# Sending inverse sums to DRAM as single elements from ScalarE's queue, without the transpose and the copy, and with all places planned anew

## The chip, the core and the metric

The kernel runs on one core of a Trainium2 chip. The metric is the device time of one execution in microseconds, as the median of several runs. A core has five engines with queues of their own: TensorE (PE, with its weight loads shown as PEld), VectorE (DVE), ScalarE (ACT), GpSimd (POOL) and SyncE (SP), and 16 DMA engines that move data between DRAM and the on-chip memory.

## What is computed

Top-k attention, then a block that expands, applies a softmax-gated unit, normalises and contracts (all float32; the two weight matrices and the gain arrive as float64).

```python
# q, k, v: (8, 8, 576, 64)
scores = scale * np.matmul(q, k.transpose(0, 1, 3, 2))
kth = np.partition(scores, -32, axis=-1)[..., -32:-31]
scores = np.where(scores >= kth, scores, -1000000000.0)
attn = np.exp(scores - np.max(scores, axis=-1, keepdims=True))
attn = attn / (np.sum(attn, axis=-1, keepdims=True) + 1e-09)
x = (attn @ v).transpose(0, 2, 1, 3).reshape(4608, 512)
h = x @ w_in                                   # 512 -> 1024
solu = h * softmax(h)
ln = (solu - mean(solu)) / np.sqrt(var(solu) + 1e-06) * g_ln
return ln @ w_out                              # 1024 -> 512
```

## The kernel before

Work is cut into 32 attention steps and 36 token groups of 128 rows. A step takes one batch and four chunks of 128 queries of two heads each, with a fifth chunk of the 64 remaining queries of both heads, so nine tiles of 128 x 576 scores. Their names: `scores` (PE) multiplies queries and keys in two row tiles of 64 rows; `evac` (ACT) copies the result from PSUM to the tile X; `count0`, `count1`, `nearest`, `best` and the `merged` stages (ACT and DVE) find the 32nd largest value; `exps` (ACT) makes E; `keep` (DVE) sets what is under the 32nd value to zero and sums each row into `den_all`; `transpose_p` (PE) and `copy_p` (ACT) turn E into PT; `attn_v` and `attn_t` (PE) multiply by the values into `om`; `copy_v` (DVE) multiplies `om` by the inverse sums and writes x, transposed. A token group then runs `mm1` (PE), `hexp` (ACT), `solu` (DVE), `square` (ACT), `spread` and `ln` (POOL), `transpose_ln` (PE), `copy_ln` (ACT), `mm2` (PE), `store` (ACT) and `send` (SP). The weights are converted from float64 at the start (`w_bits`, `w_corr` on DVE, `w_sum` on PE, `w_copy` on ACT) and read once more near the end for a check of their exponents (`w_again`, `w_exp`, `w_check`).

The way of the inverse sums is what the change touches. `inverse` (DVE) writes `rden`, 128 queries x 9 tiles. `copy_v` needs them along the free axis and the same in 64 partitions for each head, since `om` is transposed. The first three steps (`QUICK`) do this on PE (`spread_r`) and ACT (`copy_s`). The other 29 go through DRAM: `turn_r` (PE, line 2438) transposes `rden` to 9 x 128 into a `tp` buffer of PSUM, `copy_r` (ACT, line 2442) copies it into the tile `scales`, `rd_out` (SP, line 2447) stores the nine rows of 128 floats to the DRAM tile `rows`, and `rd_in` (SP, line 2456) loads them back in four broadcasts to 64 partitions each.

PSUM buffers are scarce: two of `tp` (all transposes), two of `big` (scores and mm1), two of `o` (attn_v, mm2, estimates). There is one `scales` buffer.

The order is written out ahead. `work_of` lists every operation with its engine, its cost in ns on that engine, what it comes after, which buffers it uses and how long after its start it is complete (`late`). `PLACES` gives each operation a rank. `arranged` goes through time and, on each engine, chooses among the operations that can start within `PATIENCE` of the earliest the one with the smallest rank. `TURN` is what it counts for PE's change between full-array work ("f"), row tiles ("r") and column tiles ("c"). The order that comes out is emitted as it is: each engine executes its own list in order, and semaphores hold it where data or buffers are not ready.

Of the kernel before, what the change touches and what calls it, by code (L numbers as in the profile page):

```python
# [8 lines left out]
F32 = mybir.dt.float32  # L9
# [6 lines left out]
P = 128  # L16
# [426 lines left out]
class Work:  # L443
# [6 lines left out]
    def add(self, key, engine, ns, after=(), uses=(), late=0, mode=None):  # L450
# [7 lines left out]
TURN = {("r", "f"): 150, ("f", "r"): 180, ("c", "f"): 205, ("f", "c"): 145,  # L458
        ("r", "c"): 180, ("c", "r"): 180}
# [34 lines left out]
def work_of(B, NP, steps, NF, w_wide):  # L494

    NM, NT = 4, 9
# [13 lines left out]
    for b in range(B):  # L510
        for hp in range(NP):
            n = pair(b, hp)
            add(("load_k", n), "SP", 950, behind("load_k", n), [("km", n)], late=2300)
# [11 lines left out]
    for i, (b, chunks) in enumerate(steps):  # L525
# [3 lines left out]
        add(("load_q", i), "SP", 1150, behind("load_q", i), [("q", i)], late=2300)  # L529
# [51 lines left out]
        if i in QUICK:  # L581
            for part in range(2):
                add(("spread_r", i, part), "PE", 436 if part else 654, [("inverse", i)],
                    [("small", i), ("tp", (i, "r", part))], mode="c")
                add(("copy_s", i, part), "ACT", 252 if part else 360, [("spread_r", i, part)],
                    [("tp", (i, "r", part)), ("rb", i)], 140)
        else:
            add(("turn_r", i), "PE", 109, [("inverse", i)], [("small", i), ("tp", (i, "r"))], mode="f")
            add(("copy_r", i), "ACT", 157, [("turn_r", i)], [("tp", (i, "r")), ("rb", i)], 135)
            add(("rd_out", i), "SP", 550, [("copy_r", i)], [("rows", i), ("rb", i)], 2200)  # L590
            add(("rd_in", i), "SP", 2200, [("rd_out", i)], [("rows", i), ("rb", i)], 3000)
# [108 lines left out]
def arranged(work, rank):  # L700
# [23 lines left out]
    while len(start) < len(ops):  # L724
# [56 lines left out]
        -339758, -12781, -25208, -27877, 37731, 233358, 296, 105051, 96218, 90025, 178978, 252902,  # L781
        244000, 268551, 386938, 415275, 391135, 450403, 490825, 467595, 536751, 620389, 565976,
        679127, 740719, 661851, 783898, 770731, 790228, 893927, 893785, 963266,
    ],
    "load_t": [
        -80025, -31145, 36300, 49546, 49494, 80911, 88940, 148972, 157187, 191399, 204618, 265303,
        242814, 379090, 332469, 458214, 479052, 406643, 515896, 540675, 515666, 668938, 671843,
        720581, 717982, 793192, 742027, 827758, 819520, 890032, 913039, 961682,
    ],
    "load_v": [  # L790
        5319, 1480, 51022, 45481, 188816, 144910, 179523, 153830, 308475, 246135, 333153, 327154,
        412030, 463265, 437640, 432012, 583103, 575722, 599884, 559552, 638124, 712663, 704767,
        749478, 828294, 823974, 856710, 843393, 969577, 973661, 982483, 1008016,
    ],
    "prep_t": [
        -61945, -87345, 26278, 19638, -8730, 123415, 112043, 64876, 197393, 203082, 209099,
        243285, 345702, 316325, 405050, 432741, 494037, 489994, 501941, 520044, 617082, 642835,
        681846, 688123, 761106, 717329, 792500, 787155, 909850, 920002, 957331, 948603,
    ],
    "prep_tc": [  # L800
        4338, 31729, 74439, 103211, 71892, 81529, 72919, 101742, 164515, 194340, 295053, 275591,
        364723, 341559, 415389, 407627, 461137, 438553, 503629, 486164, 631436, 665358, 673210,
        709654, 759555, 758129, 786441, 814781, 916829, 948853, 939851, 972581,
    ],
    "prep_k": [
        -60943, -63278, -70349, -26069, -42273, -8750, 127523, 59000, 243742, 222705, 246805,
        237589, 361575, 400598, 401099, 421797, 472374, 488858, 508262, 574786, 637110, 675577,
        651769, 709906, 752064, 690701, 778193, 843688, 919829, 948201, 942202, 976495,
    ],
    "prep_kc": [  # L810
        4386, 1259, 123243, 137096, 118230, 85986, 126740, 91080, 220993, 187701, 233433, 204820,
        376470, 380016, 398731, 436516, 487070, 463318, 479133, 561124, 640742, 660501, 650085,
        710914, 775148, 783534, 778524, 835240, 922803, 1013798, 954303, 988974,
    ],
    "key_square": [
        -4807, -10479, 66029, 137082, 107576, 118285, 100863, 99055, 254747, 223927, 219983,
        241887, 382074, 399900, 389837, 454608, 479887, 488157, 529275, 515189, 644860, 690979,
        690863, 719751, 737841, 761871, 779678, 864903, 916172, 907344, 975895, 1000571,
    ],
    "tail_square": [  # L820
        26929, 14605, 100013, 137131, 136063, 58308, 80392, 79370, 239575, 272229, 246883, 251581,
        308867, 311986, 422199, 446864, 515800, 468069, 496456, 535239, 638456, 682141, 683618,
        672660, 775588, 750923, 772211, 791047, 855138, 930345, 971291, 966358,
    ],
    "key_stats": [
        92348, -19748, 26035, 15202, 122190, 113992, 181544, 108957, 246207, 243025, 253021,
        288772, 408504, 419434, 373738, 411187, 494000, 466874, 543467, 571921, 654056, 667583,
        687366, 699046, 765262, 778703, 806677, 825191, 868806, 1026195, 947557, 979604,
    ],
    "load_q": [  # L830
        -59271, -10584, 162877, 208999, 217746, -8934, 78975, 113377, 212835, 187676, 290008,
        301140, 284434, 326724, 436860, 497003, 414204, 458642, 518992, 564916, 579785, 620846,
        720192, 679914, 758251, 783803, 740037, 850815, 909964, 906235, 929596, 981195,
    ],
    "prep_q": [
        -52938, -38118, 56938, 77044, -59554, 85219, 162709, 142989, 215771, 247729, 278667,
        316160, 380350, 357086, 442926, 462694, 491000, 518228, 547128, 562615, 640425, 655851,
        698990, 730851, 735544, 760091, 823699, 888865, 908286, 923741, 969433, 1014055,
    ],
    "prep_qc": [  # L840
        5438, 63366, 52446, 134767, 64136, 75161, 195035, 183808, 242849, 287460, 293191, 371510,
        425968, 364349, 488763, 476329, 465356, 525184, 499437, 614146, 626301, 699742, 698545,
        745735, 768636, 779604, 840926, 877014, 945804, 930997, 952200, 1033695,
    ],
    "query_square": [
        63169, 84418, 69142, 92064, 62677, 75066, 191341, 120686, 227118, 285294, 276140, 342226,
        401444, 383473, 418081, 451775, 479613, 516395, 563335, 580962, 631937, 667102, 657175,
        748447, 762133, 776709, 773949, 878639, 892717, 939130, 971775, 1057944,
    ],
    "estimate": [  # L850
        -83506, 127952, 79019, 27039, 105930, 180710, 89736, 42838, 243394, 306540, 313101,
        342801, 413707, 436191, 458562, 488897, 502885, 576495, 566964, 582618, 653574, 699822,
        722473, 753711, 782087, 850158, 856146, 880647, 959006, 991084, 1003644, 1011006,
    ],
    "length": [
        55390, 64287, 21492, 142925, 91820, 89828, 187422, 189102, 225343, 302444, 316321, 331213,
        430746, 450075, 467065, 483618, 443843, 521081, 600380, 589002, 638944, 706432, 747530,
        730429, 775752, 832366, 866032, 877201, 961113, 983506, 1018506, 1066670,
    ],
    "root": [  # L860
        99246, 101551, 133489, 76502, 153437, 159993, 328449, 258282, 273277, 322044, 312402,
        345682, 435376, 421796, 426558, 489636, 494032, 574332, 622205, 621698, 663835, 788227,
        724548, 699723, 787574, 869704, 806750, 895189, 992785, 957593, 981899, 1024982,
    ],
    "begin": [
        11137, 56722, 26318, 141798, 82875, 187369, 201720, 176412, 273406, 321410, 278640,
        361581, 425447, 451800, 489085, 488954, 519027, 611009, 600940, 647109, 684366, 701264,
        752228, 758419, 793179, 851495, 882821, 921112, 988338, 1009069, 981779, 1020470,
    ],
    "scores": [  # L870
        [-59418, -45149, -46228, -36187, -85715, -39882, -83465, -59766, -61961],
        [82657, 60941, 68216, 26269, 63090, 61996, 26242, 61177, 58723],
        [87860, 87901, 87890, 62437, 67835, 57982, 159959, 48482, 69765],
        [84367, 83743, 155862, 144031, 34877, 75359, 128841, 135567, 145817],
        [71537, 53849, 68902, 132976, 59114, 118037, 68873, 110264, 107915],
        [141646, 97925, 94716, 134455, 142943, 99507, 191485, 186882, 96824],
        [152938, 191224, 59110, 197551, 203891, 215510, 127964, 202152, 197201],
        [226026, 229460, 237313, 237035, 187502, 187736, 192780, 199624, 198798],
        [269141, 275943, 254553, 254580, 277300, 269126, 277259, 275937, 249924],
# [358 lines left out]
        787847, 845540, 871626, 909493, 924810, 1042553, 1016671, 1060191, 1094822, 1099148,  # L1238
    ],
    "spread_r": [  # L1240
        [61416, 70137],
        [85209, 91923],
        [131370, 129488],
    ],
# [539 lines left out]
def fast_path(  # L1784
# [29 lines left out]
    NM = 4  # L1814
# [929 lines left out]
```

## Time and profile before

| | |
|---|---|
| median of 3 runs | 1195.1 us (1193.06 to 1195.21) |
| profiled execution | 1193.35 us |
| its span, first to last instruction | 1191.5 us |
| granted TensorE clock, mean | 0.991 |
| PE, DVE, ACT, POOL busy | 1143.5, 1054.0, 1014.4, 154.4 us |
| DMA packets | 110408, 64.55 MB |
| `rd_out`, the store of nine rows, on SP | 29 issues, 300 ns each (median) |
| `rd_in`, the broadcasts, on SP | 116 issues, 588 ns each (median) |
| `inverse`, first reciprocal, on DVE | 32, 196 ns each (mean) |

The profile is of one execution. A group's row gives line, engine, operation, the tiles written and read, the shapes and the count; then the busy time in us and the mean duration of one in ns; then the time for which the engine was idle just before these instructions, and what ended it. Matmuls overlap in the array, so the duration of one is longer than the distance between two starts; the timeline's start times give the distance. DMA-issuing instructions appear on the queue of the engine that issues them (SPq) and do not count as busy; the time of the record is that of the issue, and the landing comes later.

### The profile page before, as it was taken

The numbers are of one execution on the slowest core, as the hardware profiler recorded it, in microseconds if no ns is written. First come the engines' busy times: TensorE is split into PE (matmuls) and PEld (weight loads), VectorE is DVE, ScalarE is ACT, GpSimd is POOL, SyncE is SP. The second block draws the span as 40 slices with busy tenths as digits, with TensorE's granted clock in tenths as the row PEclk, the third lists the DMA queues.
The fourth block names the chain that finished last, engine by engine and source line by source line (L and its number), as shares of the span: only waits on it lengthen the run. The fifth ranks groups of instructions, "written<-read, shape, count | busy, mean of one in ns | idle before, by whom it ended". The sixth has DMA issues, their size and how long they took to land.

```text
span 1191.5 us, 18863 instructions
## 1 busy us (share of the span) xinstructions
PE 1143.5 (96%) x5868; PEld 648.2 (54%) x5868; DVE 1054.0 (88%) x3113; ACT 1014.4 (85%) x2180; POOL 154.4 (13%) x169
## 2 busy tenths in 40 slices
PE   6689999999999999999999999999999999999997
PEld 3345455555555555555555655555555555555553
DVE  4999999999899999899979998899989888999821
ACT  7899798999988898999896998999877989988642
POOL 1101101102021020202031010211013001120110
PEclk9799999999999999999999999999999999999999
DMA  7323111012110122111120112111020101102521
GB/s 202 97 75 92 43 34 48 13 49 54 59 26 28 33 63 65 37 45 40 51 54 12 40 49 68 31 41 52 30 76 18 42 21 40 59 11 91 173 76 30
DMA packets 110408, 64.55 MB, mean 54 GB/s; under 512 B 89421, under 2 KB 97882, under 8 KB 110298
## 3 DMA queue, kind: packets, MB, share of 16 engines
q1 hardware_dynamic: 110298, 63.25, 18.8%
q8 instruction: 49, 0.80, 0.3%
q14 instruction: 61, 0.50, 0.1%
HBM read 53.65 MB, written 9.57 MB: 53 GB/s over the span
## 4 chain that ended last, share of the span: by engine, by line
PE 50%; DVE 27%; ACT 17%; issue 3%; POOL 2%; DMA 0%; DVEq 0%; ACTq 0%; POOLq 0%
PE o_ps L2628 14%; PE h_ps L2567 9%; PE s_ps L2216 9%; ACT sg L2291 7%; PE tp_p L2470 6%; PE om L2526 6%; DVE junkv L2234 6%; DVE w L2323 5%; DVE w L2312 5%; DVE E L2393 3%; ACT PT L2483 2%; DVE solu L2586 2%; ACT X L2227 2%; PE tp_ln L2617 2%; PE om L2535 2%
## 5 line engine op out<-in xcount | busy, mean ns | idle before, releaser
L2628 PE MATMUL o_ps<-w_out,lnT 128*128 128x512 f32 x576 | 258.2, 594 | 0.2
L2567 PE MATMUL h_ps<-w_in,xTm 128*128 128x512 f32 x512 | 229.2, 593 | 0.0
L2323 DVE MAX8 w<-w 128x8 f32<-128x288 f32 x576 | 223.3, 445 | 0.2
L2291 ACT ACTIVATE sg<-X,t 128x576 bf16<-128x576 f32 x256 | 196.4, 774 | 12.0 <-DVE t L2276 10.8
L2312 DVE SCALAR_TENSOR_TENSOR w<-X,al,sg 128x576 f32<-128x576 f32 x256 | 200.7, 813 | 0.8
L2393 DVE SCALAR_TENSOR_TENSOR E<-X,kth,E 128x576 f32<-128x576 f32 x256 | 199.1, 815 | 1.6
L2227 ACT ACTIVATE X<-s_ps 128x576 f32<-128x576 f32 x256 | 160.2, 661 | 25.0 <-PE s_ps L2216 22.5
L2234 DVE TENSOR_SCALAR_CACHE_REDUCE junkv<-X,t 128x576 bf16<-128x576 f32 x216 | 174.6, 808 | 7.6 <-ACT X L2227 1.5
L2216 PE MATMUL s_ps<-kT,qT 64*128 64x288 f32 x1024 | 169.1, 438 | 9.8 <-ACT X L2227 4.4
L2628 PEld LDWEIGHTS o_ps<-w_out,lnT 128*128 128x128 f32 x576 | 105.1, 190 | 112.4 <-issue 110.1
L2470 PE MATMUL tp_p<-ident,E 128*128 128x128 f32 x1024 | 153.1, 278 | 7.9 <-DVE E L2393 2.9
L2483 ACT COPY PT<-tp_p 128x512 f32<-128x512 f32 x256 | 147.0, 591 | 12.4 <-PE tp_p L2470 11.9
L2470 PEld LDWEIGHTS tp_p<-ident,E 128*128 128x128 f32 x1024 | 116.3, 141 | 65.4 <-issue 31.8
L2348 ACT ACTIVATE E<-X 128x1152 f32<-128x1152 f32 x128 | 149.1, 1183 | 1.4 <-PE tp_p L2470 1.2
L2567 PEld LDWEIGHTS h_ps<-w_in,xTm 128*128 128x128 f32 x512 | 93.3, 190 | 98.1 <-issue 95.7
L2526 PE MATMUL om<-PT,vm 128*64 128x320 f32 (+1 forms) x1024 | 136.1, 411 | 1.0 <-ACT osb L2635 0.9
L2186 POOL TENSOR_TENSOR zs<-zs,phalf 128x9 f32<-128x9 f32 x32 | 63.6, 1989 | 520.2 <-DVE zs L2180 520.2
L2216 PEld LDWEIGHTS s_ps<-kT,qT 64*128 64x128 f32 x1024 | 85.7, 186 | 68.3 <-issue 22.2
L2526 PEld LDWEIGHTS om<-PT,vm 128*64 128x64 f32 x1024 | 69.9, 136 | 54.6 <-issue 10.6
L2602 POOL TENSOR_SCALAR var<-var 128x1 f32<-128x1 f32 x36 | 13.0, 361 | 490.3 <-ACT e_sb L2596 490.1
L2596 ACT ACTIVATE e_sb<-solu,nmu 128x1024 f32<-128x1024 f32 x36 | 41.5, 1153 | 23.1 <-DVE nmu L2590 21.8
L2578 ACT ACTIVATE e_sb<-h_ps 128x1024 f32<-128x1024 f32 x36 | 36.7, 1020 | 20.0 <-PE h_ps L2567 19.7
(146 smaller groups left out, 1503.9 us busy)
## 6 DMA issues: line engine op xcount, KB each, us to landing
km<-in_k_dram SPq DMA_DIRECT2D x32, 256.0 KB
q_sb<-in_q_dram SPq DMA_DIRECT2D x64, 128.0 KB
vm<-in_v_dram SPq DMA_DIRECT2D x32, 256.0 KB
out_dram<-osb SPq DMA_DIRECT2D x32, 256.0 KB
scales<-rows SPq DMA_DIRECT2D x58, 128.0 KB
w_raw<-in_moe_w_in_dram SPq DMA_DIRECT2D x8, 512.0 KB
w_raw<-in_moe_w_out_dram SPq DMA_DIRECT2D x8, 512.0 KB
w_again<-in_moe_w_in_dram SPq DMA_DIRECT2D x8, 512.0 KB
```

Of the source, the lines that this page charges most:

```text
L2216: nc.tensor.matmul(out=s[:, n, 0:SH], lhsT=queries_of(i, t)[hd, :], rhs=kT[hd, k0 : k0 + SH], start=True, stop=True,)
L2227: nc.scalar.activation(out=x, in_=st[i].pop(("s", j))[:, :, 0:SH], func=AF.Copy, scale=scale,)
L2234: nc.vector.tensor_scalar(out=junk, in0=x_of(i, j), scalar1=st[i][t][:, j : j + 1], scalar2=None, op0=ALU.is_ge, op1=ALU.add, accum_out=co ...
L2291: nc.scalar.activation(out=d["sg", j], in_=x_of(i, j), func=AF.Sign, scale=-(1.0 + 2.0**-23), bias=d["t1"][:, j : j + 1], accum_out=column ...
L2312: nc.vector.scalar_tensor_tensor(out=w, in0=x_of(i, j), scalar=d["al"][:, j : j + 1], in1=d.pop(("sg", j)), op0=ALU.subtract, op1=ALU.mult,)
L2323: nc.vector.max(w8[:, j, 8 * half : 8 * half + 8], w[:, half * SH : (half + 1) * SH])
L2393: nc.vector.scalar_tensor_tensor(out=e, in0=x_of(i, j), scalar=d["kth"][:, j : j + 1], in1=e, op0=ALU.is_ge, op1=ALU.mult, accum_out=den_a ...
L2470: nc.tensor.transpose(tp[:, c, :], e[:, c * P : (c + 1) * P], ident)
L2483: nc.scalar.copy(out=dst, in_=st[i].pop(("tp", j)))
L2526: nc.tensor.matmul(out=o[h * D : (h + 1) * D, cols], lhsT=vm[:, h, c, :], rhs=pt[:, h * NM + c, :], start=(c == 0), stop=False,)
L2567: nc.tensor.matmul(out=h[:, half, :], lhsT=x[:, c, :], rhs=w_in[:, c, half * 512 : (half + 1) * 512], start=(c == 0), stop=(c == NP - 1),)
L2628: nc.tensor.matmul(out=o, lhsT=d["lnT"][:, c, :], rhs=w_out[:, c, :], start=(c == 0), stop=(c == NF - 1),)
```

## The change

`turn_r` and `copy_r` go. `rd_out` is issued by ACT and reads `rden` as it lies, one float per partition and tile, and writes each float to its place in `rows`; the tile `scales` is made in `rd_in`. The list of work drops the two operations and gives `rd_out` a cost of 120 ns on ACT and a completion 11.5 us later. Some other constants of the planner change (`TURN`, `PATIENCE`, the completion of the key and query loads), and every entry of `PLACES` is new, so the order of all engines differs from the first instructions on. What each operation computes stays the same.

```diff
-TURN = {("r", "f"): 150, ("f", "r"): 180, ("c", "f"): 205, ("f", "c"): 145,
-        ("r", "c"): 180, ("c", "r"): 180}
+TURN = {("r", "f"): 240, ("f", "r"): 165, ("c", "f"): 205, ("f", "c"): 145,
+        ("r", "c"): 270, ("c", "r"): 170}
...
-            add(("load_k", n), "SP", 950, behind("load_k", n), [("km", n)], late=2300)
+            add(("load_k", n), "SP", 950, behind("load_k", n), [("km", n)], late=2900)
...
-        add(("load_q", i), "SP", 1150, behind("load_q", i), [("q", i)], late=2300)
+        add(("load_q", i), "SP", 1150, behind("load_q", i), [("q", i)], late=2600)
...
-            add(("turn_r", i), "PE", 109, [("inverse", i)], [("small", i), ("tp", (i, "r"))], mode="f")
-            add(("copy_r", i), "ACT", 157, [("turn_r", i)], [("tp", (i, "r")), ("rb", i)], 135)
-            add(("rd_out", i), "SP", 550, [("copy_r", i)], [("rows", i), ("rb", i)], 2200)
+            add(("rd_out", i), "ACT", 120, [("inverse", i)], [("rows", i), ("small", i)], 11500)
             add(("rd_in", i), "SP", 2200, [("rd_out", i)], [("rows", i), ("rb", i)], 3000)
...
     "load_k": [
-        -339758, -12781, -25208, -27877, 37731, 233358, 296, 105051, 96218, 90025, 178978, 252902,
+        -742416, -129654, 665, 17427, 61193, 38197, 82610, 76745, 143063, 127915, 287541, 271748,
...
-PATIENCE = {"PE": 300, "ACT": 100, "DVE": 100, "POOL": 100, "SP": 2000}
+PATIENCE = {"PE": 1000, "ACT": 1000, "DVE": 1000, "POOL": 1000, "SP": 4000}
...
-    def turn_r(i):
-        tp = st[i]["tp_r"] = ps_tp.tile([P, NM, P], F32, tag="tp", name="tp_r")
-        nc.tensor.transpose(tp[0:NT, 0, :], st[i]["rden"], ident)
-
-    def copy_r(i):
-        st[i]["scales"] = p1.tile([P, S], F32, tag="scales", name="scales")
-        nc.scalar.copy(out=st[i]["scales"][0:NT, 0:P], in_=st[i]["tp_r"][0:NT, 0, :])
-
     def rd_out(i):
 
         rows = st[i]["rows"] = dram.tile([NT, P], F32, tag="rows", name="rows")
-        nc.sync.dma_start(out=rows, in_=st[i]["scales"][0:NT, 0:P])
+        nc.scalar.dma_start(out=rows.rearrange("j p -> p j"), in_=st[i]["rden"])
 
     def rd_in(i):
 
         rows = st[i]["rows"].rearrange("j p -> (j p)")
-        scales = st[i]["scales"]
+        scales = st[i]["scales"] = p1.tile([P, S], F32, tag="scales", name="scales")
         for cols, n in ((slice(0, SM), SM), (slice(SM, S), ST)):
```

## The prediction

> **What bounds the kernel now.** I read the page first, then the busy time by stage, then TensorE's waits, then the timelines where the changed instructions stand.
>
> ```profile
> span 1191.5 us, 18863 instructions
> PE 1143.5 (96%) x5868; PEld 648.2 (54%) x5868; DVE 1054.0 (88%) x3113; ACT 1014.4 (85%) x2180; POOL 154.4 (13%) x169
> ```
>
> TensorE is busy for 96% of the span, which a mean over stages could still hide something under. The stages (time, then PE, PEld, DVE, ACT, POOL busy, PE clock, DMA share, GB/s):
>
> ```profile
> 0.00:50.00 50.00, 33.40 (x146) 17.84 (x147) 33.05 (x89) 38.72 (x91) 5.20 (x31) 0.90 0.63 167
> 50.00:100.00 50.00, 39.14 (x263) 23.72 (x264) 48.05 (x147) 46.71 (x103) 3.64 (x2) 0.93 0.23 67
> 150.00:400.00 250.00, 246.74 (x1309) 141.47 (x1308) 237.59 (x707) 221.97 (x473) 32.81 (x28) 1.00 0.15 40
> 400.00:800.00 400.00, 397.50 (x2102) 229.15 (x2099) 368.78 (x1096) 359.15 (x778) 56.72 (x51) 1.00 0.17 44
> 800.00:1140.00 340.00, 335.94 (x1735) 192.19 (x1733) 308.58 (x914) 288.35 (x605) 44.15 (x41) 1.00 0.20 60
> ```
>
> From 150 to 1140 us PE is idle for 9.8 of 990 us. All other idle PE time is at the ends: 27.5 us in the first 100, 7.7 in the last 52 (the verdict and the final stores). So the end is set by the PE work that the order contains, plus what the order makes PE wait; DVE (92% in the middle) and ACT have some room. An edit is worth what it takes off PE. Microseconds off ACT, SP or DVE count only if PE waits for them.
>
> **The change, part by part.**
>
> *The turn.* 29 steps (the 32 less the three quick ones) lose one transpose of `rden` on PE and one copy on ACT.
>
> ```profile
> L2438 PE MATMUL tp_r<-ident,rden 128*9 128x128 f32 x29 | 7.9, 274 | 0.8 <-ACT PT L2483 0.8
> L2442 ACT COPY scales<-tp_r 9x128 f32<-9x128 f32 x29 | 7.1, 244 | 4.1 <-PE tp_r L2438 4.1
> ```
>
> 274 ns is a latency; matmuls overlap. In the timeline the turn starts at 1112.26 and the next transpose at 1112.37: it takes 0.11 us of PE's order, so 29 x 0.11 = 3.2 us go. The copy on ACT starts at 1128.45 and the next instruction at 1128.61: 0.16 x 29 = 4.6 us of ACT go, off the path. The turn also gives back one of the two `tp` buffers 29 times.
>
> *The new places.* I compared the built order of both kernels. DVE and POOL keep the same instructions; SP loses 29 issues, ACT has 29 issues for 29 copies. What the places change on PE is how the row-tiled scores (64 rows, line 2216) are mixed with full-array work. Starts in PE's timeline give the price of that mixing:
>
> ```profile
> 60.88 0.60 PE L2470 MATMUL tp_p<-ident,E 128*128 128x128 f32 x4
> 61.41 0.76 PE L2216 MATMUL s_ps<-kT,qT 64*128 64x288 f32 x4
> 62.10 1.09 PE L2470 MATMUL tp_p<-ident,E 128*128 128x128 f32 x8
> ...
> 96.88 1.24 PE L2216 MATMUL s_ps<-kT,qT 64*128 64x288 f32 x8
> 98.05 0.66 PE L2470 MATMUL tp_p<-ident,E 128*128 128x128 f32 x4
> ...
> 982.54 1.24 PE L2216 MATMUL s_ps<-kT,qT 64*128 64x288 f32 x8
> 984.05 1.30 PE L2216 MATMUL s_ps<-kT,qT 64*128 64x288 f32 x8 [0.27 <-ACT X L2227]
> ```
>
> One scores operation (x4) between others takes 62.10 - 61.41 = 0.69 us, two (x8) take 98.05 - 96.88 = 1.17, so one more costs 0.48 and leaving the row-tiled form costs 0.69 - 0.48 = 0.21. Entering it costs 61.41 - 60.88 - 4 x 0.11 = 0.09. A separate run of scores costs 0.3 us beyond its work. The old order has 145 such runs, the new one 125: 20 x 0.3 = 6.0 us less. Column-tiled runs (attn_v) go from 55 to 56, nothing.
>
> Against it: scores have two `big` buffers, so the third operation of a run waits until ACT has evacuated the first. Two 16-matmul runs of the old order, one of them at 982.54 above, last 2.74 us from first start to the next other matmul; 4 x 0.48 + 0.21 = 2.13 was the work, so such a run pays 0.6 us. A 12-matmul run pays the same. Behind the first 100 us of PE work the old order has 3 runs of over two operations, the new one 15, two of them of 6 and 8: 12 x 0.6 = 7.2, and 0.3 for the longest two. That is 7.5 us if all of it is new. Short runs wait for `X` too: the scores show 24.0 us of waits for ACT X in 55 waits (mostly of weight loads, which overlap), so a merged run partly moves a wait. Bounds 0 and 7.5; I take two thirds, 5.0, because the measured 0.6 us is the nearest row. Runs of PE groups that fill both `tp` buffers are a little shorter in the new order: -0.5.
>
> *The issue on ACT.* `rd_out` moves from SP (line 2447) to ACT and becomes 128 x 9 single elements, 1152 pieces instead of 9. ACT's queue shows no DMA before, so I bound it by SP's: SP was held 0.30 us for the 9-piece store and 0.64 us for the key load, which has 128 x 8 pieces of 256 B. The nearest by pieces is the key load.
>
> ```profile
> 0.72 0.77 SPq L2034 DMA_DIRECT2D km<-in_k_dram  x1
> ...
> 307.94 0.30 SPq L2447 DMA_DIRECT2D rows<-scales  x1
> 309.23 2.93 SPq L2456 DMA_DIRECT2D scales<-rows  x4
> ...
> 388.54 0.64 SPq L2034 DMA_DIRECT2D km<-in_k_dram  x1
> ```
>
> If ACT stands still for 0.65 us at each, less the copy's 0.16, it is 0.49 x 29 = 14.2 us of ACT. The Trainium skill ("Advanced Engine Details and Errata", Engine Queue Depths) gives ScalarE a queue of 8 instructions. With those ahead the sequencer issues while the engine works, and the price is nearly 0. No run here shows ACT issuing. By the row the sum would be up to +14.2 us, by the rule 0. I take 0, since ACT is busy for 88% of the middle with instructions of 0.6 to 1.2 us, and keep the other end. The issue also waits for `inverse` on DVE, and what stands behind it on ACT (mostly a PSUM copy that PE needs, or a count) waits too.
>
> *The landing.* The old chain was turn, copy, store, and 1.29 us after the store's issue SP issued the broadcast (307.94 to 309.23). The key load issued at 0.72 let PE start at 4.28, 3.6 us for about as many pieces, so from that row the elements land in about 4 us. The skill speaks against this form: "DMA: Bandwidth & Descriptors", Rules for kernel authors, says a non-contiguous last dimension becomes one descriptor per element and should be rearranged; its Specifications say that pieces under 512 B are read, modified and written. So it may be several times slower; the new plan allows 11.5 us. What covers it is DVE's work between `inverse` and the first `copy_v` that needs the result. Counted in the new order with the durations of the rows it is 20 to 48 us for steps 3 to 30. Four broadcast issues take 2.4 us and their landing is no longer than the key load's 3.6, so any landing under 20 - 6 = 14 us is hidden: by row and by rule 0. At the last step DVE has only 7.0 us of work there, but PE has about 19 us of other work between that issue's place and the first matmul of the last tokens, again more than 11.5 + 6. SP now waits at the broadcast for the landing, 4 to 11.5 us instead of 1.3, and value, query and tail loads stand behind it; SP idles for most of the time and loses 29 x 0.30 us of issues. Nothing added. The elements share the DMA engines, 15 to 20% busy in the middle.
>
> *The start.* Weights are loaded sooner, the second step's queries later (SP's order); the work in front of the first mm1 is 65 us of PE in the old order and 66 in the new. I take 0, with 5 us either way.
>
> **Sum**: -3.2 - 6.0 + 5.0 - 0.5 = -4.7 us, ends -9.7 and -2.2 by the long runs alone. The profiled execution took 1193.35 us (span 1191.5 and 1.9 around it), which gives 1188.65. It stands 1.75 us under the median of the three runs, 1195.1, so against the median the forecast is 1190.4.
>
> **Rivals.**
> 1. *ACT pays for the issue* (slower side). Each of the 29 issues holds ACT up to 0.49 us net just where a PSUM copy is due; PE waits for it because `tp` and `big` have two buffers each. PE has no slack from 150 us on, so most of it would be added. It cancels the gain at 4.7 / 29 = 0.16 us each, and is slower beyond the measurable from 7.1 / 29 = 0.24. For it: 1152 pieces, the 0.64 us row, and PSUM copies behind many issues. Against: the queue rule, and that ACT idles for 12% there. At 0.4 us each: 1190.4 + 11.6 = 1202.
> 2. *The order itself waits more.* The long runs cost their full 7.5, the start loses 5 to 8 us, since DVE is busy for 48 of 50 us from 50 on and later queries delay it: 1190.4 + 2.5 + 7 = 1199.9. For it: in the first 100 us every order decides 27.5 us of PE idle time. Against: the landmarks (mm1, attn_v, copy_v) stand at nearly the same work in both.
> 3. *The elements land late*, beyond 14 us. `copy_v` then holds DVE, and PE behind it. At 18 us the short-covered third of the steps lose some 3 us each: 10 x 3 = 30, half of it regained: 1190.4 + 15 = 1205.
> 4. *Nothing is left*: long runs cancel runs saved, 1194.
>
> **Numbers.** This kernel's measurement can tell about 0.2%, 2.4 us, from no change. My forecast 0.60 (of it 0.45 faster, 0.12 within, 0.03 slower; own range 1184 to 1196), rival 1: 0.17, rival 2: 0.15, rival 3: 0.06, rival 4: 0.02. So faster 0.45, same 0.14, slower 0.41. The range goes down to 1182, the sum's good end (1185.4) with part of the start's 5 us, and up to 1206, which takes in rivals 1 and 2; that leaves 2 in 10 outside.
>
> **What would show it.** Right: PE busy about 3 to 9 us less, no row tp_r at 9 columns, PE idle from 150 to 1140 us still near 10, waits of scores for ACT X some 5 us longer. Wrong: PE idle in the middle of 20 us or more; named by ACT copies behind the rows issue, rival 1; by X, rival 2; DVE's copies into xTm waiting for a DMA, rival 3. In the ACT timeline the gap around the issue gives its price; the time from it to SP's broadcast gives the landing.

## The result and the profile after

The change made the kernel slower: 1244.55 us (median of 4 runs, 1243.92 to 1245.11) against 1194.46 us for the kernel before on the same chip. The ratio is 1.0418, 95% interval 1.0405 to 1.0430, so +50 us where -4.7 was forecast. The page of the kernel after:

```profile
span 1242.6 us, 18669 instructions
PE 1152.0 (93%) x5838; PEld 650.3 (52%) x5839; DVE 1070.5 (86%) x3113; ACT 1021.0 (82%) x2151; POOL 150.7 (12%) x169
```

TensorE's busy time did not fall by 3 to 9 us, as the prediction's sign of being right asked, it rose by 8.5, and its share fell from 96% to 93%: it stands more. The stages (columns as before: PE, PEld, DVE, ACT, POOL busy, PE clock, DMA share, GB/s):

```profile
0.00:50.00 50.00, 31.49 (x155) 17.50 (x156) 34.72 (x95) 40.12 (x93) 5.20 (x31) 0.86 0.65 173
50.00:100.00 50.00, 39.21 (x271) 24.11 (x270) 48.16 (x149) 45.07 (x102) 3.58 (x2) 0.97 0.24 67
150.00:400.00 250.00, 241.08 (x1266) 137.64 (x1266) 236.24 (x688) 218.45 (x455) 30.91 (x28) 1.00 0.22 41
400.00:800.00 400.00, 392.36 (x2062) 225.35 (x2061) 369.31 (x1080) 355.36 (x749) 55.12 (x51) 1.00 0.20 44
800.00:1140.00 340.00, 312.74 (x1577) 178.26 (x1575) 291.95 (x852) 273.01 (x567) 37.30 (x35) 0.96 0.20 37
```

From 150 to 1140 us PE idles for 43.8 us instead of 9.8, and 27 of them lie behind 800 us. There the clock is 0.96 as well, and DVE and ACT fall back together with PE. The sign that the prediction set for itself ("PE idle in the middle of 20 us or more") is there. The names come from the waits. The SP queue's own at the broadcast, before and after (us in total, times, longest), then those of the engines after that a DMA ended:

```profile
SPq L2456 <- DMA rows<-scales: 23.1, 22, 1.7
```

```profile
SPq L2436 <- DMA rows<-rden: 414.3, 29, 29.6
```

```profile
PE pre L2064 <- DMA qk_tails<-in_q_dram: 14.8, 4, 5.6
...
ACT osb L2615 <- DMA out_dram<-osb: 13.8, 5, 9.4
DVE xTm L2529 <- DMA scales<-rows: 13.6, 1, 13.6
```

In the kernel before, the longest such wait outside SP, beside the first key load's 4.3 us, was 1.0 us. And the DMA rows give the landing, the last column being the median time from issue to landing over those issues for which the trace has a landing (8 of the 29 for `rows`):

```profile
scales<-rows SPq DMA_DIRECT2D x58, 128.0 KB, 3.8
...
rows<-rden ACTq DMA_DIRECT2D x29, 4.5 KB, 11.8
```

A store of 4.5 KB takes 11.8 us. Two places show how that reaches TensorE. The first is the timeline around 820 us (start, duration; idle time before it and what ended it in brackets):

```profile
803.42 0.36 SPq L2619 DMA_DIRECT2D out_dram<-osb  x1
805.80 0.37 ACTq L2427 DMA_DIRECT2D rows<-rden  x1
818.16 2.37 SPq L2436 DMA_DIRECT2D scales<-rows  x4
820.63 1.18 SPq L2032 DMA_DIRECT2D qk_tails<-in_q_dram  x2
...
823.87 0.82 PE L2064 MATMUL pre<-ident,qk_tails 128*128 128x128 f32 x2 [4.29 <-DMA qk_tails<-in_q_dram]
```

SP issues nothing from 803.8 to 818.2: it stands at the broadcast until the elements have landed. The tail load behind it goes out at 820.63, and PE waits 4.3 us for it. The broadcast itself had time; what was hurt is the neighbour behind it. The second place, around 1040 us:

```profile
1036.06 0.37 ACTq L2427 DMA_DIRECT2D rows<-rden  x1
1037.16 0.58 ACT L2615 COPY osb<-o_ps 128x512 f32<-128x512 f32 x1
1037.77 0.36 SPq L2619 DMA_DIRECT2D out_dram<-osb  x1
...
1050.31 0.59 ACT L2615 COPY osb<-o_ps 128x512 f32<-128x512 f32 x1 [9.38 <-DMA out_dram<-osb]
...
1052.60 4.37 PE L2204 MATMUL s_ps<-kT,qT 64*128 64x288 f32 x16 [8.29 <-ACT kT L2091]
```

Here SP is in time. It issues the output store 1.7 us after the elements. Such stores land in 2.7 us (median of the recorded ones); this one frees its buffer `osb` only 12.5 us after its issue (1037.77 to 1050.31). ACT needs that buffer, stands for 9.4 us, and PE stands for 8.3 behind it. After such a stall PE also runs slowly for a while. The same stretch of time in the kernel after, and then in a variant with the same order (first experiment):

```profile
1052.60:1058.00 5.40, 5.40 (x21) 3.29 (x22) 4.25 (x19) 3.09 (x5) 0.00 (x0) 0.50 0.34 102
```

```profile
1052.60:1058.00 5.40, 5.40 (x23) 2.61 (x23) 5.37 (x14) 5.18 (x10) 1.12 (x3) 1.00 0.00 2
```

The clock column reads 0.50 and 1.00. Behind the three stalls of PE between 800 and 1140 us that last 4.3, 5.6 and 8.3 us the clock is at 0.50 for 6.8, 6.8 and 10.2 us, and behind one of 2.5 us it stays at 1.00. The Trainium skill ("TensorE: Matmul & The Clock Gate", Part 1: The HAM clock gate) puts the clock at half after an idle window of about 3.4 us; this trace agrees, while in the third experiment a stall of 2.8 us, too, was followed by 3.4 us at 0.50. The three stretches are 12 us' worth of clock, partly in time when PE stood anyway.

One sentence ahead of the prediction has to be mended: four engines execute the list that `arranged` writes, but line 2676 names only these four, and SP's list is placed by the framework.

### The profile page after: what moved, and what is told of

Its sections match the earlier page's. It is cut to its first block, busy times and chain, and to the rows that moved or that the text cites. A ratio compares the mean times of both kernels' runs of the same rounds, so it can differ in the third digit from the quotient of the medians.

```text
span 1242.6 us, 18669 instructions
## 1 busy us (share of the span) xinstructions
PE 1152.0 (93%) x5838; PEld 650.3 (52%) x5839; DVE 1070.5 (86%) x3113; ACT 1021.0 (82%) x2151; POOL 150.7 (12%) x169
## 5 line engine op out<-in xcount | busy, mean ns | idle before, releaser
L2311 DVE MAX8 w<-w 128x8 f32<-128x288 f32 x576 | 227.9, 448 | 3.1
L2582 POOL TENSOR_SCALAR var<-var 128x1 f32<-128x1 f32 x36 | 9.9, 275 | 559.2 <-ACT e_sb L2576 559.1
L2603 ACT COPY lnT<-tp_ln 128x512 f32<-128x512 f32 x72 | 41.2, 591 | 14.8 <-PE tp_ln L2597 14.7
L2589 POOL TENSOR_SCALAR solu<-solu,nmu,rstd 128x1024 f32<-128x1024 f32 x36 | 52.7, 1464 | 3.8
```

What stands on the lines that cost most here:

```text
L2311: nc.vector.max(w8[:, j, 8 * half : 8 * half + 8], w[:, half * SH : (half + 1) * SH])
```

## The experiments

Three theories. A: SP stands at the broadcast, and what stands behind it comes late. B: the new places themselves make PE wait. C: the element writes delay the completion of other DMAs, whoever waits. "Ratio" is to the kernel before, with its 95% interval.

**1. The landing alone** (`e6_rows36`). One access pattern is changed; all five lists stay exactly the same. The values then lie in DRAM in another order, and the queries are multiplied by each other's inverse sums: this variant, and those below that use its store, do not give the right result and serve for their time alone.

```diff
-        nc.scalar.dma_start(out=rows.rearrange("j p -> p j"), in_=st[i]["rden"])
+        nc.scalar.dma_start(out=rows.rearrange("j p -> (j p)").rearrange("(p j) -> p j", j=NT), in_=st[i]["rden"])
```

> The kernel after with one access pattern changed: ScalarE stores the inverse sums as 128 pieces of 36 bytes (one for each partition) instead of 1152 single elements. The order of the instructions is the same on all engines. The values lie in DRAM in another order, so the queries are multiplied by each other's inverse sums. Three theories. A: SP stands at the broadcast until the elements have landed (11.8 us, median), and what stands behind it on SP's queue comes late. B: the new places themselves make TensorE wait. C: the single-element writes delay the completion of other DMAs, whoever waits. A and C expect the landing at 2 to 4 us and 1186 to 1200 us; SP's waits for rows fall from 414 to under 150 us. B expects 1235 to 1245 us.

1206.58 us, ratio 1.0095 (1.0078 to 1.0111). The landing row and SP's list at the first place:

```profile
rows<-rden ACTq DMA_DIRECT2D x29, 4.5 KB, 1.4
```

```profile
803.51 0.36 SPq L2619 DMA_DIRECT2D out_dram<-osb  x1
807.34 2.37 SPq L2436 DMA_DIRECT2D scales<-rows  x4
813.77 1.11 SPq L2032 DMA_DIRECT2D qk_tails<-in_q_dram  x2
```

The broadcast goes out at 807.34 instead of 818.16 and the tail load 6.9 us earlier. Of the ratio 1.0418, 0.0323 is due to the single elements in this order: 0.0323 x 1194.5 = 38.6 us. What is left, 0.0095 or 11.3 us, is not. That SP's list is the same in both also says that the framework placed the broadcasts without regard to whether the landing takes 1.4 or 11.8 us.

**2. Elements that nobody waits for** (`e7_rows36_and_elements`). Behind each 36-byte store ACT issues the 1152 elements too, into a tile that nobody reads.

```diff
+        rows, more = [dram.tile([NT, P], F32, tag=t, name=t) for t in ("rows", "more")]
+        nc.scalar.dma_start(out=rows.rearrange("j p -> (j p)").rearrange("(p j) -> p j", j=NT), in_=st[i]["rden"]); st[i]["rows"] = rows; nc.scalar.dma_start(out=more.rearrange("j p -> p j"), in_=st[i]["rden"])
```

> As the run with 36-byte pieces, and right behind each such store ScalarE issues the 1152 single elements too, to a DRAM tile that nobody reads. SP waits for the 36-byte store alone. A expects what the run with 36-byte pieces gives, within 4 us (29 more issues of 0.37 us on ScalarE are hidden). C expects at least half of the loss to come back, over 1215 us, with broadcasts, loads and stores of outputs issued within 12 us of the elements landing at 8 us or more instead of 3.

1241.44 us, ratio 1.0402 (1.0365 to 1.0438): almost all of the loss is back. The DMA rows:

```profile
scales<-rows SPq DMA_DIRECT2D x58, 128.0 KB, 12.0
...
rows<-rden ACTq DMA_DIRECT2D x29, 4.5 KB, 1.4
more<-rden ACTq DMA_DIRECT2D x29, 4.5 KB, 11.9
```

The store that SP waits for lands in 1.4 us, but the broadcasts behind the elements, on another queue, land when the elements do. In the middle (150 to 1140 us), SP's DMAs issued within 8 us after elements have a median landing of 11.6 us (15 with a recorded landing), all others 2.5 us (28). C holds; A alone does not explain the loss.

The trace's records of single DMA packets say what is late. In the kernel after, the elements' own packets take 7 ns each (median), and the last of them starts 1.7 us behind the issue (median), ten microseconds ahead of the landing. But 181 of the data packets of SP's DMA queue between 150 and 1140 us take over 1 us, up to 8.5; all of them start within 14 us behind an element store. In this second experiment there are 271. The kernel before has 2 and the first experiment 1, none over 1.3 us. So it is data that is held up, and not only the report of its landing.

**3. The edit alone in the old order** (`e2_edit_alone`). The old ranks and constants; where the copy stood on ACT, the element store is issued.

```diff
...
     def copy_r(i):
-        st[i]["scales"] = p1.tile([P, S], F32, tag="scales", name="scales")
-        nc.scalar.copy(out=st[i]["scales"][0:NT, 0:P], in_=st[i]["tp_r"][0:NT, 0, :])
...
         rows = st[i]["rows"] = dram.tile([NT, P], F32, tag="rows", name="rows")
-        nc.sync.dma_start(out=rows, in_=st[i]["scales"][0:NT, 0:P])
+        nc.scalar.dma_start(out=rows.rearrange("j p -> p j"), in_=st[i]["rden"])
...
```

> The kernel before with its own ranks and constants, and the edit alone: no turn and no copy, and where the copy stood on ScalarE the store of single elements is issued there. The list of TensorE loses only the turns. A and C expect SP's waits for rows of 300 us or more instead of 23, and 1215 to 1260 us. B expects 1188 to 1196 us, since the order is the old one.

1278.08 us, ratio 1.0701 (1.0677 to 1.0725), more than either A or C foresaw. SP's waits for rows are 427.8 us in 28 times, and now `copy_v` waits too: 57.6 us in 13 times for the broadcasts, where the new order has one such wait. The new places did what they were planned for, to cover the 11.5 us for DVE; B as the whole cause falls. With elements in both, the new order is 1278.08 - 1244.55 = 33.5 us faster than the old one.

**4. The old order with a short landing** (`e12_old_order_rows36`). As the third, with the store of the first.

> The old order with the edit alone, the store as 128 pieces of 36 bytes in place of single elements: the turn and the copy are gone, the landing is short, and no place is new. B in part (the new places cost the 11 us that the 36-byte run in the new order keeps over the kernel before) expects 1188 to 1196 us. If the edit itself cost them (the issue on ScalarE, or the longer landing of a store that no copy precedes), 1203 us or more.

1190.84 us, ratio 0.9974 (0.9966 to 0.9982): the removal of the turn and the copy, with the short store in place of SP's, is worth 0.0026 x 1194.2 = 3.1 us. The page:

```profile
span 1188.5 us, 18680 instructions
PE 1139.4 (96%) x5839; PEld 648.3 (55%) x5839; DVE 1053.4 (89%) x3113; ACT 1008.8 (85%) x2151; POOL 154.5 (13%) x169
```

Against it, the first experiment has the same edit and the new places: 1.0095 - 0.9974 = 0.0121, or 14.5 us, is their cost. The three steps on the way from the kernel before to the one after are -3.1 + 14.5 + 38.6 = 50.0 us. Another way has other parts: in the old order the elements cost 1.0701 - 0.9974 = 0.0727, or 87 us.

**5. The new order with the turn** (`e1_turn_back`). Turn, copy and nine-row store from SP are put back into the new order where a `tp` buffer is free.

> The kernel after with its own ranks and constants, and the turn, the copy and the store of nine rows from SP put back where the element store stood (or a little later, once a tp buffer and the tile scales are free). This is the new order without the edit. A and C expect 1188 to 1203 us (29 turns of 0.11 us and some of their turnarounds are back). B expects 1235 us or more.

1227.66 us, ratio 1.0267 (1.0249 to 1.0284), between the two expectations. Inserted turns take `tp` buffers that the order had not planned for, and SP stands 232.8 us in 28 waits at the store for the copy into `scales`. It tells nothing apart.

**6. and 7. SP planned for the landing** (`e5_sp_written`, `e8_sp_written_rows36`). SP's list is taken from the planner too, which counts 11.5 us; once with elements, once with 36-byte pieces.

```diff
-    with tc.manual_schedule(engines={E.PE, E.Activation, E.DVE, E.Pool}):
+    with tc.manual_schedule(engines={E.PE, E.Activation, E.DVE, E.Pool, E.SP}):
```

> The kernel after with one line changed: SP's list is taken from the planner too, as the lists of the other four engines are, instead of being placed by the framework. The planner counts 11.5 us for the landing, so the broadcasts stand later on SP, with other loads ahead of them. A (SP's stand at the broadcast is what costs) expects SP's waits for rows under 200 us instead of 414, and 1203 to 1218 us. C (the elements delay the completion of other DMAs, whoever waits) expects 1228 us or more.

> As the run with SP's list from the planner, with the store of 128 pieces of 36 bytes in place of the 1152 single elements; all five lists are the same as there. Its time says what SP's new list is worth without the elements, and the difference of the two what the elements cost where SP is planned for them. A expects the two within 6 us of each other, C this one at least 20 us faster.

1225.97 us, ratio 1.0257 (1.0230 to 1.0284), and 1208.04 us, ratio 1.0115 (1.0098 to 1.0132): the first between the two expectations, the two 18 us apart, also between, but nearer to C's. SP's waits for rows in the one and the other:

```profile
SPq L2436 <- DMA rows<-rden: 157.5, 19, 22.9
```

```profile
SPq L2436 <- DMA rows<-rden: 39.7, 7, 13.5
```

They fall from 414.3 to 157.5 us, and that recovers 0.0161, or 19 us, of the loss, although more of SP's DMAs are now issued within 8 us behind elements (49 instead of 20 in the middle): with the first place above, that speaks for A's part in the kernel after, though the new list changes more than the stands. The other 0.0142, 17 us, stays. In it, 18 of SP's DMAs with a recorded landing behind elements land at 7.1 us (median), which is C; but with the short store the same list waits for 39.7 us only, so some of SP's stands are left as well. These two runs do not split the 17 us.

**8. Elements issued late** (`e11_elements_late`). The first experiment, and ACT issues 1152 unread elements ahead of `copy_v`, when the step's own broadcasts are out.

```diff
+            if kind == "copy_v" and args[1] == 0 and args[0] not in QUICK:
+                more = dram.tile([NT, P], F32, tag="more", name="more")
+                nc.scalar.dma_start(out=more.rearrange("j p -> p j"), in_=den_all[:, args[0], :])
```

> The 36-byte run in the new order (1206.6 us), with 1152 single elements stored in addition, which nobody reads or waits for, in each of the 29 steps: ScalarE issues them ahead of the first copy_v of the step, when the step's own broadcasts have been issued, from den_all. SP never stands for them and the broadcasts of the same step are mostly ahead of them. A expects within 4 us of 1206.6. C expects over 1215 us, with loads, broadcasts or output stores issued up to 10 us after the elements landing at 6 us or more.

1238.01 us, ratio 1.0367 (1.0349 to 1.0384). Nobody waits for these stores and they add 31 us, so C is enough for most of the loss, though it lengthens SP's waits for rows, too (from 156.0 to 215.5 us). PE now waits for query loads (12.0 us in three waits) and DVE for broadcasts (19.2 us in two).

**9. and 10. What is slow about the elements** (`e14_spread64`, `e15_column`). The eighth with only the destination, then only the number of elements changed; PE's and SP's lists stay the same. Against the two lines of the eighth: first the elements 64 bytes apart (`e14_spread64`), then the one column (`e15_column`).

```diff
-                more = dram.tile([NT, P], F32, tag="more", name="more")
-                nc.scalar.dma_start(out=more.rearrange("j p -> p j"), in_=den_all[:, args[0], :])
+                more = dram.tile([NT, P, 16], F32, tag="more", name="more")
+                nc.scalar.dma_start(out=more[:, :, 0].rearrange("j p -> p j"), in_=den_all[:, args[0], :])
...
+                more = dram.tile([1, P], F32, tag="more", name="more")
+                nc.scalar.dma_start(out=more.rearrange("j p -> p j"), in_=den_all[:, args[0], 8:9])
```

> As the run with unread single elements ahead of copy_v (1238.0 us; elements landing at 10.3 us), with the same 1152 single elements on places 64 bytes apart instead of side by side; all lists are the same. Two reasons for the slow landing: D, the number of 4-byte pieces for each DMA engine, expects the landing at 9 us or more and 1230 to 1240 us; E, that many engines write 4 bytes each into the same stretch of DRAM one after another, expects a landing under 5 us and 1206 to 1215 us.

> As the run with unread single elements ahead of copy_v, with one column of 128 single elements side by side instead of nine (8 pieces for each DMA engine). D expects a landing under 3 us, as for 128 pieces of 36 bytes, and 1206 to 1211 us. E expects 7 us or more (in the run with 16-byte pieces the one column landed at 8.3 us, behind the other store) and 1220 us or more.

1207.11 us, ratio 1.0110 (1.0093 to 1.0127), and 1235.21 us, ratio 1.0345 (1.0328 to 1.0362). The landing rows of the one and the other:

```profile
more<-den_all ACTq DMA_DIRECT2D x29, 4.5 KB, 3.2
```

```profile
more<-den_all ACTq DMA_DIRECT2D x29, 0.5 KB, 8.3
```

The same 1152 elements 64 bytes apart land in 3.2 us and cost nothing that can be told from noise beside the first experiment's 1206.58 (ratios 1.0110 and 1.0095, with intervals that overlap). A ninth of them, 128 side by side, take 8.3 us and cost 29 us. SP's data packets of over 1 us follow: 48 in the eighth experiment, 0 and 105 in these two. D falls, E holds in what can be seen: it is 4-byte writes next to each other in DRAM, not their number. Which unit makes them wait for each other these runs do not show.

**11. and 12. Two versions that keep the whole computation**, both in the old order. In `e13_pieces16` each head's four sums of a query go out as one 16-byte piece, the ninth column as single elements, and `copy_v` reads `scales` with a stride. In `e16_read_turned` the sums go out as 36-byte pieces, SP reads them back as single elements into nine partitions, and the nine rows are stored and broadcast as before. First the lines of the one, then of the other:

```diff
+        nc.scalar.dma_start(
+            out=flat[0 : 2 * SM].rearrange("(h p t) -> p h t", h=2, t=NM),
+            in_=rden[:, 0 : 2 * NM].rearrange("p (h t) -> p h t", h=2),
+        )
+        nc.scalar.dma_start(out=flat[2 * SM :].rearrange("(p o) -> p o", o=1), in_=rden[:, 2 * NM : NT])
...
+        nc.scalar.dma_start(out=st[i]["pieces"], in_=st[i]["rden"])
+        nc.sync.dma_start(out=s[0:NT, 0:P], in_=st[i]["pieces"].rearrange("p j -> j p"))
+        nc.sync.dma_start(out=rows, in_=s[0:NT, 0:P])
```

> A version that keeps the whole computation, in the old order: no turn and no copy; ScalarE stores, for each head, the four inverse sums of a query as one piece of 16 bytes (256 pieces) and the ninth column as 128 single elements; the broadcasts read whole stretches as before, and copy_v reads scales with a stride of four. 384 pieces are 24 for each DMA engine, where 36-byte pieces were 8 (landing 1.4 us) and single elements 72 (11.8 us); in proportion that is a landing of 4.0 us. The old order with the turn gone took 1190.8 us with 36-byte pieces; a landing of 4 us delays few other DMAs: 1190 to 1195 us, and under 1193 it is faster than the kernel before. If any store of many pieces holds other DMAs to a cost in proportion (38 us for 72 pieces an engine), 10 us come on top: 1200 us.

> A version that keeps the whole computation in the old order, without the turn and without single elements written side by side to DRAM: ScalarE stores 128 pieces of 36 bytes to DRAM (1.4 us), SP reads them as 1152 single elements into nine partitions of scales, and from there the nine rows are stored and broadcast as in the kernel before. If only small writes side by side in DRAM are slow, reading single elements lands in 2 to 5 us, other DMAs land as before, and the time is 1189 to 1196 us; under 1192.4 it beats the kernel before. If reading single elements is as slow as writing them, or SP's two more waits in each step hold its loads, 1205 us or more.

1222.43 us, ratio 1.0243 (1.0218 to 1.0268), and 1209.87 us, ratio 1.0138 (1.0121 to 1.0155): neither beats the kernel before. The two stores of the first version, then `copy_v` in the kernel before and in this version:

```profile
rows<-rden ACTq DMA_DIRECT2D x29, 4.0 KB, 1.9
rows<-rden ACTq DMA_DIRECT2D x29, 0.5 KB, 8.3
```

```profile
L2549 DVE TENSOR_TENSOR xTm<-om,scales 128x256 f32<-128x256 f32 x64 | 26.7, 418 | 13.0 <-PE om L2535 12.7
```

```profile
L2558 DVE TENSOR_TENSOR xTm<-om,scales 128x256 f32<-128x256 f32 x64 | 38.1, 597 | 17.5 <-PE om L2538 11.7 <-DMA scales<-rows 5.5
```

The sum by pieces for each DMA engine (4.0 us) was wrong, and this run, made before the ninth and tenth, led to them: 256 pieces of 16 bytes land in 1.9 us, the 128 single elements in 8.3. The strided read also takes 597 ns where the old row had 418; how the 29 us of loss divide between the two is not shown. In the second version the longer chain is the likely price: no packet of SP's takes over 1 us, but `copy_v` waits for the broadcasts again, and SP stands for the extra hop.

```profile
DVE xTm L2550 <- DMA scales<-rows: 20.7, 8, 11.8
```

```profile
SPq L2448 <- DMA scales<-pieces: 78.0, 27, 4.2
```

78.0 / 27 = 2.9 us that SP waits for the elements it has just asked for: reading single elements is not slow in the way that writing them side by side is.

## Why the prediction was wrong

- *The turn, -3.2 us*: right. The fourth experiment measures -3.1 us (-2.1 to -4.1 by its interval) with the turn, the copy and SP's store gone; the latency of 274 ns in place of the start-to-start distance would have given -7.9.
- *The issue on ACT, 0 against up to +14.2*: right. One issue takes 0.37 us, and 29 more of them (ninth experiment) cost 0.5 us by the medians and 1.8 by the ratios, within the noise. What the prediction concluded from the depth of the queue, that ACT works on while it issues, holds here, and rival 1 falls.
- *The landing, about 4 us*: failed. The key load's row was near by number of pieces, but it writes to SBUF, and each piece has 256 bytes. The deciding property, 4-byte writes side by side in DRAM, no row of the trace of before had, and the range of 4 to 11.5 us should have been carried through every later step.
- *"Any landing under 14 us is hidden"*: right for what it was said of. In the order it was counted in, `copy_v` waited once, at the last step (13.6 us, PE 5.0), where the prediction had counted on PE's other work to cover it.
- *"Nothing added" for SP and the DMA engines*: the step that failed, and 38.6 us hang on it. The prediction named the waiting instruction (SP at the broadcast, up to 11.5 us) and the queue behind it (value, query and tail loads), and then set the cost to zero because SP idles for most of the time. A queue's idle time is no cover when a load behind the stand has less lead (the time from its turn to the need for its data) than the stand takes, as the tail load issued at 820.63 had. It also did not ask whose transfers the slow writes hold. The late landings (11.6 us behind elements against 2.5 elsewhere) fit what the Trainium skill ("DMA: Bandwidth & Descriptors", Queues, rings and completion order) says, that a completion's increment lands only after every earlier write of the same DMA engine, across its queues; but the packet records show the data of these transfers held too, so that rule is not the whole of it. Its size rule cited in the prediction (pieces under 512 B are read, modified and written) did not decide: 36-byte pieces landed in 1.4 us.
- *The new places, -6.0 + 5.0 - 0.5 = -1.5 us*: mis-sized; 14.5 us measured. For the scores the mechanism was right. Adding up PE's starts behind 100 us in the first and the fourth experiment, runs fall from 127 to 108, the steps into them take 29.1 instead of 35.0 us and the runs 147.1 instead of 142.8, together -1.6. The runs of over two operations cost 10.2 us more over their price than the old order's, where 5.0 was taken and 7.5 the bound. The rest lies in other work, set to zero: PE's visible waits grow from 40.0 us in 57 to 48.8 in 80, none of the new ones over 5 us, and a token's first `mm1` comes later by 1 us at the first, 7 at 260 us, 13 at 750 and 16 at the end. That is rival 2's kind of loss, spread thinner and larger: 16 us over the forecast's term instead of its 9.5. Which of the new ranks cause it stays open.
- *Rivals*: rival 3 had the late landing, but as a wait of `copy_v`; the loss came in the main through DMAs that have nothing to do with the inverse sums. The copy's one such wait, 13.6 us, came at the last step.
- *Idle time of PE before*: the prediction put all of it outside the middle at the ends; 3.5 us more lie between 100 and 150 us, which changes nothing in the sum.

## What to carry to other kernels

Price a DMA that is made slower by its neighbours: list what stands behind the wait on the issuing queue with each one's lead (how long before its use it is issued), and treat every transfer issued before the slow one has landed as landing with it, on whichever queue. Before a store is cut into small pieces, ask where the pieces lie in DRAM; one run with the same instructions and another destination pattern tells what the pieces cost. A planner's estimate helps only on the engines whose list it writes.

## What the hardware showed that was not expected

- 128 single floats side by side in DRAM took 8.3 us to land and 1152 took 11.8, while 1152 floats 64 bytes apart took 3.2, 256 pieces of 16 bytes 1.9 and 128 pieces of 36 bytes 1.4.
- A slow store on ACT's queue made loads, broadcasts and stores issued on SP's queue behind it land late (11.6 us instead of 2.5), reads of DRAM included, and single packets of theirs took up to 9.1 us; in the kernel before and with the short store the longest took 1.3.
- PE's clock reads 0.50 behind a stall of 8.3 us in the middle of the kernel, and 1.00 at the same place without the stall.
